# Top-k attention and a GELU MLP in one kernel: q and k turned in 32x32 squares by the vector engine, and top-k over lists of the larger and smaller of key pairs

## The chip, the cores and the metric

The kernel runs on one core of a Trainium2 chip. The core has five engines that run their own instruction queues in order and meet only at semaphores: TensorE (PE; its weight loads are listed as PEld), VectorE (DVE), ScalarE (ACT), GpSimd (POOL) and SyncE (SP, which here only issues DMAs). The metric is the device time of one execution in microseconds, the median over several runs. Lower is better.

## What is computed

Attention over 8 batches, 8 heads, 576 tokens and 64 features, in which every query keeps the 32 largest of its 576 scores; its output, 4608 tokens by 512 features, goes through an MLP with an exact GELU. All data are float32.

```python
scores = scale * np.matmul(q, k.transpose(0, 1, 3, 2))      # (8, 8, 576, 576)
kth = np.partition(scores, -top_k, axis=-1)[..., -top_k:-top_k + 1]   # top_k = 32
mask = scores >= kth
scores = np.where(mask, scores, -1000000000.0)
scores = scores - np.max(scores, axis=-1, keepdims=True)
attn = np.exp(scores)
attn = attn / (np.sum(attn, axis=-1, keepdims=True) + 1e-09)
out = np.matmul(attn, v)
...
x = out.transpose(0, 2, 1, 3).reshape(4608, 512)
h = x @ w_in                                                # (4608, 2048)
g = 0.5 * h * (1.0 + erf(h * inv_sqrt2))
return g @ w_out                                            # (4608, 512)
```

## The kernel before

**Pairs and items.** Two heads of one batch make a pair: 32 pairs, 4 to a batch, so that two heads of 64 features fill 128 partitions. The 576 tokens of a head are four blocks of 128 and a tail of 64 (`NM` = 4, `SM` = 512, `TL` = 64). An item is one block of queries of one pair, both heads side by side (scores of 128 x 1152); the tails of two pairs together make one item more. That gives 18 items a batch, 144 in all. Batches with an even number have their tail items last, the others first.

**Slots.** The main loop (L940 on) runs over slots n. The order of each engine's queue is the order in which the program text issues, written out by hand. In slot n the kernel issues, in this order: the scores of item n+2 (PE, copied to SBUF by ACT), the product of attention and v for item n-3 (PE), the softmax of item n-1 (ACT), the transposes of item n-2's weights (PE, copied by ACT), between them pieces of the MLP (PE), and "prep" pieces that transpose q and k of a later pair; then, at the end of the slot, `top_k(n)` (DVE), `threshold(n)` (POOL), `normalise(n-1)` (POOL) and small additions of the MLP (POOL). From slot 13 on (`few`) the order within a slot is: the tail transposes of item n-2 with the last keys of item n+2, one MLP piece, the other transposes, the first prep piece, the second half of the softmax of item n-1, `add_small(n-1)`, the remaining prep pieces, the rest of the MLP pieces.

**The lines that matter.**

- `load` (L87 to L98) brings q, k or v of one pair to SBUF through SP's queue: four DMAs, two per head, with tokens on the partitions and runs of 64 features. q and k have two buffers each, v five.
- `transpose_qk` (L246 to L273) turns one pair's q and k, features to the partitions, in three pieces: k's four blocks; the two tails; q's four blocks. Each piece is 2 to 4 transposes on PE into a PSUM bank (L263), and a copy by ACT to `kt` or `qm` (L268; the first pair's by DVE). The third piece then issues the loads of the pair two further on. `kt` (tails first, then 512 columns of k) has six buffers, `qm` four. `slots_of` (L928) says in which slot, counted from the batch's first, each piece goes.
- `scores` and `last_keys` (L298 to L362) multiply them; `last_keys` of a tail item is L317.
- `top_k` (L364 to L386) takes the 32 largest of each row: four rounds of MAX8 (L378), which gives the eight largest of 576, and between them three of MATCH_REPLACE8 (L381), which writes a very low number over those eight, each for both heads. After the last MAX8 it issues `inverse(n-1)`, the reciprocal of item n-1's sums (L404).
- `threshold` (L393, L396) makes the two biases of the softmax from the first and the 32nd value; `softmax` (L417, L418) applies them, and its second instruction also sums a row up into `den`; `add_small` (L410) adds 1e-9 to `den`; `normalise` (L431) multiplies with the reciprocals, on POOL in one instruction of 128 x 1152.

So there is a loop from slot to slot: softmax of item n-1, `den`, reciprocal on DVE, `normalise` on POOL, transposes on PE in slot n+1, their copy on ACT, the next softmax behind it on ACT.

- The MLP's first layer is L594, its second L676, L694, L730 and L732, its GELU L610; POOL's part in it is L625 to L628 and L753 to L797. How many of its pieces a slot takes is fixed by `room_in`; it begins at slot 11, as `START` is 10. What is left when the last item is through runs at the end.

Of the kernel before, what the change touches and what calls it, by code (L numbers as in the profile page):

```python
# [8 lines left out]
TOPK = 32  # L9
# [5 lines left out]
def kernel(  # L15
# [55 lines left out]
    xT = const.tile([P, KO, COLS], f32, name="xT")  # L71


    raws = {n: [const.tile([P, NJ, 2, D], f32, name=f"raw_{n}{i}") for i in range(m)]
            for n, m in (("k", 2), ("q", 2), ("v", NP + 1))}
# [11 lines left out]
    def load(n, pair, queue=None, queue2=None):  # L87
        if pair >= n_pairs:
            return
        queue = queue or nc.sync  # L90
        queue2 = queue2 or queue
        b, h0 = pair // NP, 2 * (pair % NP)
        t, src = raw_of(n, pair), sources[n]
# [151 lines left out]

    def transpose_qk(pair, first=False):  # L246

        rq, rk = raw_of("q", pair), raw_of("k", pair)
        groups = {
            0: [(rk, j) for j in range(NM)],  # L250
            1: [(rq, NM), (rk, NM)],
            2: [(rq, j) for j in range(NM)],
        }

        def piece(c):
            if c == 0:
                kt_of[pair] = work.tile([P, 2 * P + SM], f32, tag="kt", bufs=NP + 2, name="kt")
            if c == 2:
                q_of[pair] = work.tile([P, SM], f32, tag="qm", bufs=NP, name="qm")
            tp = bank("tp_qk")  # L260
            n = len(groups[c]) * P
            for x, (r, j) in enumerate(groups[c]):
                nc.tensor.transpose(  # L263
                    tp[:, x * P : (x + 1) * P], r[:, j].rearrange("p e d -> p (e d)"), ident
                )
            dst = q_of[pair] if c == 2 else kt_of[pair][:, 2 * P :] if c == 0 else kt_of[pair][:, 0 : 2 * P]
            copy = nc.vector.tensor_copy if first and c < 2 else nc.scalar.copy
            copy(out=dst, in_=tp[:, 0:n])  # L268
# [29 lines left out]
    def last_keys(i, t_ps):  # L298

        pair, t = items[i]  # L300
        s = S_of[i]
        if t < NM:
            nc.tensor.matmul(  # L303
                t_ps[:, 0:P], lhsT=q_of[pair][:, t * P : (t + 1) * P],
                rhs=kt_of[pair][:, P : 2 * P], start=True, stop=True,
            )
            if i == 0:
                return lambda: nc.vector.tensor_scalar(
                    s[:, SM : S + TL], t_ps[:, 0:P], scale, None, op0=ALU.mult
                )  # L310
            return lambda: nc.scalar.activation(
                s[:, SM : S + TL], t_ps[:, 0:P], func=AF.Copy, scale=scale
            )
        for r in range(2):
            kt = kt_of[pair + r]
            for e in range(2):
                nc.tensor.matmul(  # L317
                    t_ps[half(r, e), r * TL : (r + 1) * TL],
                    lhsT=kt[:, e * TL : (e + 1) * TL],
                    rhs=kt[:, P + e * TL : P + (e + 1) * TL],  # L320
                    start=True, stop=True,
                )
        return lambda: nc.scalar.activation(
            s.rearrange("p (r n) -> p r n", r=2)[:, :, SM:S],
            t_ps[:, 0:P].rearrange("p (r n) -> p r n", r=2), func=AF.Copy, scale=scale,
        )

    def scores(i):
        if i >= N:
            return  # L330
        pair, t = items[i]
        S_of[i] = s = work.tile([P, 2 * S], f32, tag="s", bufs=5, name="s")
        s_ps = pair_tile("s_ps")
        if not few[0]:
            last_keys(i, bank("t_ps"))()
        if t < NM:
            q_t, kt = q_of[pair][:, t * P : (t + 1) * P], kt_of[pair]
            for c in range(2):
                for e in range(2):
                    rows = slice(e * D, (e + 1) * D)  # L340
                    nc.tensor.matmul(  # L341
                        s_ps[:, e, c * 256 : (c + 1) * 256], lhsT=q_t[rows, :],
                        rhs=kt[rows, 2 * P + c * 256 : 2 * P + (c + 1) * 256], start=True, stop=True,
                    )
            if i == 0:

                nc.scalar.activation(s[:, 0:SM], s_ps[:, 0], func=AF.Copy, scale=scale)  # L347
                nc.scalar.activation(s[:, S + TL :], s_ps[:, 1], func=AF.Copy, scale=scale)  # L348
                return
            nc.scalar.activation(spread(s, S + TL, SM), s_ps, func=AF.Copy, scale=scale)  # L350
        else:

            for r in range(2):
                kt = kt_of[pair + r]
                for e in range(2):
                    rows = slice(e * D, (e + 1) * D)
                    nc.tensor.matmul(  # L357
                        s_ps[half(r, e), r, :], lhsT=kt[rows, e * TL : (e + 1) * TL],
                        rhs=kt[rows, 2 * P :], start=True, stop=True,
                    )  # L360
# [3 lines left out]
    def top_k(i, hooks):  # L364


        stat_of[i] = st = {
            "top": work.tile([P, 2, TOPK], f32, tag="top", name="top"),
            "neg": work.tile([P, 2, 2], f32, tag="neg", name="neg"),
            "bias": work.tile([P, 2], f32, tag="bias", name="bias"),  # L370
            "den": work.tile([P, 2], f32, tag="den", name="den"),
            "rden": work.tile([P, 2], f32, tag="rden", name="rden"),
        }
        cur = [row(i, e) for e in range(2)]
        rest = work.tile([P, 2, S], f32, tag="rest", bufs=1, name="rest")
        for r in range(TOPK // 8):
            for e in range(2):
                nc.vector.max(st["top"][:, e, 8 * r : 8 * r + 8], cur[e])  # L378
            if r < TOPK // 8 - 1:
                for e in range(2):  # L380
                    nc.vector.match_replace(  # L381
                        rest[:, e], st["top"][:, e, 8 * r : 8 * r + 8], cur[e], LOWEST
                    )
                cur = [rest[:, e] for e in range(2)]
            if r in hooks:
                hooks.pop(r)()  # L386

    def threshold(i):

        if i < 0 or i >= N:  # L390
            return
        st = stat_of[i]
        nc.gpsimd.tensor_scalar(  # L393
            st["neg"], st["top"][:, :, 0 :: TOPK - 1], -1.0, None, op0=ALU.mult
        )
        nc.gpsimd.tensor_tensor(  # L396
            st["bias"], st["neg"][:, :, 0], st["neg"][:, :, 1], op=ALU.subtract
        )

    def inverse(i):  # L400
        if i < 0 or i >= N:
# [10 lines left out]
    def softmax(i, e):  # L412

        if i < 0 or i >= N:
            return
        st, s = stat_of[i], row(i, e)
        nc.scalar.activation(s, s, func=AF.Prelu, bias=st["neg"][:, e, 1:2], scale=1.0, alpha=STEEP)  # L417
# [101 lines left out]
    def attend(i):  # L519
# [420 lines left out]
    for n in range(ahead):  # L940
# [78 lines left out]
        run_small(6)  # L1019
# [7 lines left out]
        if n <= NP:  # L1027
            load("v", n)

    ready[0], left[0] = NT, len(pieces)  # L1030
# [36 lines left out]
```

## Time and profile before

| what | before |
|---|---|
| median of 3 runs | 1609.99 us (1609.68 to 1610.74) |
| the profiled execution | 1609.49 us |
| its span in the profile | 1607.7 us |
| PE clock granted, mean | 0.996 |
| L594 PE, first layer | 560.7 us, x2560 |
| L378 DVE MAX8, 128x576 | 811.5 us, x1152, 743 and 748 ns each |
| L381 DVE MATCH_REPLACE8, 128x576 | 635.4 us, x864, 743 and 744 ns each |
| L263 PE transposes of q and k | 56.8 us, x320 |
| L268 ACT copies of them | 18.7, 18.1 and 11.5 us |
| L431 POOL `normalise` | 293.0 us, x139, 2108 ns each |
| L404 DVE reciprocal | 22.8 us, x144, and 112.4 us idle before it, for POOL's `den` L410 |
| q and k loads on SP's queue | x64 and x62 of 128 KB, as many of 16 KB, landing after 2.1 to 2.5 us |

"Busy" of a group is the time in which at least one of its instructions runs; as neighbours overlap on DVE and PE, it is less than their number times the mean. Idle time before a group is put down to what ended it. A float32 matmul has two records in the trace, so the numbers of PE's groups for the products are twice those in the program.

### The profile page before, as it was taken

How to read it: one execution, taken by the hardware profiler on the slowest of the kernel's cores; microseconds unless marked ns; L12 is line 12 of the kernel's file. 1: busy time of each engine (PE TensorE's matmuls, PEld its weight loads, DVE VectorE, ACT ScalarE, POOL GpSimd, SP SyncE). 2: the span in 40 equal slices, each digit the busy share in tenths (PEclk: the TensorE clock that was granted, in tenths of full speed). 3: DMA queues.
4: the chain of work that ended last, by engine and by line, in shares of the span. 5: the costliest groups of instructions: out<-in, count | busy, mean ns of one | idle time of the engine just before them, and what ended most of it. 6: DMA issues, size and time to landing. Idle time of an engine off the chain costs nothing.

```text
span 1607.7 us, 27629 instructions
## 1 busy us (share of the span) xinstructions
PE 1568.1 (98%) x10032; PEld 1262.7 (79%) x10032; DVE 1415.5 (88%) x3052; ACT 1205.0 (75%) x2122; POOL 774.1 (48%) x1044
## 2 busy tenths in 40 slices
PE   7899999999999999999999999999999999999998
PEld 6776678888787778888787778888878777888787
DVE  8999989989999889998999888998999988999800
ACT  6989877777778777777777877777777877777730
POOL 4775766534544445433454535443454444543442
PEclk9999999999999999999999999999999999999999
DMA  6523210011100110011110111001110011000000
GB/s 167 150 92 115 83 43 1 14 37 38 23 14 16 43 41 19 1 29 37 31 29 16 29 30 44 1 14 37 38 23 14 16 29 23 14 1 14 8 14 13
DMA packets 126920, 56.31 MB, mean 35 GB/s; under 512 B 117792, under 2 KB 118336, under 8 KB 126784
## 3 DMA queue, kind: packets, MB, share of 16 engines
q1 hardware_dynamic: 125520, 54.12, 12.5%
q8 instruction: 79, 1.29, 0.3%
q10 hardware_dynamic: 1200, 0.39, 0.1%
q14 instruction: 57, 0.47, 0.1%
q0 software_dynamic: 64, 0.03, 0.0%
HBM read 45.08 MB, written 9.44 MB: 34 GB/s over the span
## 4 chain that ended last, share of the span: by engine, by line
PE 89%; DVE 9%; ACT 2%; POOL 1%; issue 0%; DVEq 0%; POOLq 0%
PE h_ps L594 31%; PE y_ps L732 19%; PE o L538 8%; PE s_ps L341 7%; PE tp L481 7%; DVE top L378 5%; DVE rest L381 4%; PE seven L730 3%; PE tp_qk L263 2%; PE tp_t L303 2%; PE y_ps L694 2%; PE y_ps L697 2%; PE y_ps L676 2%; PE s_ps L357 1%; PE o L549 1%; PE tp_t L455 1%
## 5 line engine op out<-in xcount | busy, mean ns | idle before, releaser
L378 DVE MAX8 top<-rest 128x8 f32<-128x576 f32 x864 | 609.7, 748 | 0.0
L594 PE MATMUL h_ps<-xT,w_in_sb 128*128 128x256 f32 (+1 forms) x2560 | 560.7, 363 | 1.0 <-ACT g L610 1.0
L594 PEld LDWEIGHTS h_ps<-xT,w_in_sb 128*128 128x128 f32 x2560 | 428.8, 190 | 82.6 <-issue 32.3
L381 DVE MATCH_REPLACE8 rest<-top,rest 128x576 f32<-128x576 f32 x576 | 423.6, 743 | 0.0
L410 POOL TENSOR_SCALAR den<-den 128x2 f32<-128x2 f32 x144 | 32.0, 222 | 656.3 <-ACT s L418 656.2
L431 POOL TENSOR_TENSOR s<-s,rden 128x1152 f32<-128x1152 f32 x139 | 293.0, 2108 | 0.3 <-DVE rden L404 0.3
L418 ACT ACTIVATE s<-s,bias 128x576 f32<-128x576 f32 x288 | 223.4, 776 | 12.6
L417 ACT ACTIVATE s<-s,neg 128x576 f32<-128x576 f32 x288 | 224.4, 779 | 0.1
L381 DVE MATCH_REPLACE8 rest<-top,s 128x576 f32<-128x576 f32 x288 | 211.8, 744 | 0.0
L497 ACT COPY pt<-tp 128x1024 f32<-128x1024 f32 x133 | 134.5, 1011 | 97.2 <-PE tp L481 96.9
L378 DVE MAX8 top<-s 128x8 f32<-128x576 f32 x288 | 201.8, 743 | 1.4 <-ACT s L347 1.4
L350 ACT ACTIVATE s<-s_ps 128x1024 f32<-128x1024 f32 x127 | 130.4, 1027 | 73.9 <-PE s_ps L341 62.0
L538 PE MATMUL o<-pt,raw_v 128*64 128x256 f32 x1280 | 154.3, 386 | 0.4 <-ACT pt L488 0.4
L481 PE MATMUL tp<-ident,s 128*128 128x128 f32 x1152 | 149.6, 273 | 0.0
L341 PE MATMUL s_ps<-kt,qm 64*128 64x256 f32 x1024 | 147.1, 406 | 0.8 <-ACT s L348 0.8
L481 PEld LDWEIGHTS tp<-ident,s 128*128 128x128 f32 x1152 | 134.6, 141 | 14.8 <-issue 2.1
L732 PE MATMUL y_ps<-w_out_sb,sum 128*128 128x256 f32 x480 | 142.8, 379 | 0.0
L538 PEld LDWEIGHTS o<-pt,raw_v 128*64 128x64 f32 x1280 | 87.1, 137 | 63.9 <-issue 19.9
L341 PEld LDWEIGHTS s_ps<-kt,qm 64*128 64x128 f32 x1024 | 89.1, 188 | 45.4 <-issue 27.1
L732 PE MATMUL y_ps<-w_out_sb,g 128*128 128x256 f32 x480 | 122.5, 379 | 0.0
L404 DVE RECIPROCAL rden<-den 128x2 f32<-128x2 f32 x144 | 22.8, 159 | 112.4 <-POOL den L410 111.9
L732 PEld LDWEIGHTS y_ps<-w_out_sb,sum 128*128 128x128 f32 x480 | 91.2, 190 | 12.4
(132 smaller groups left out, 2176.2 us busy)
## 6 DMA issues: line engine op xcount, KB each, us to landing
raw_q<-in_q_dram SPq DMA_DIRECT2D x64, 128.0 KB, 2.4
raw_v<-in_v_dram SPq DMA_DIRECT2D x64, 128.0 KB, 2.4
raw_k<-in_k_dram SPq DMA_DIRECT2D x62, 128.0 KB, 2.5
out_dram<-y SPq DMA_DIRECT2D x30, 256.0 KB, 2.1
w_out_sb<-in_moe_w_in_dram SPq DMA_DIRECT2D x14, 511.8 KB, 4.9
w_out_sb<-in_moe_w_out_dram SPq DMA_DIRECT2D x10, 511.8 KB, 4.3
w_sum<-in_moe_w_out_dram SPq DMA_DIRECT2D x6, 511.8 KB, 4.3
out_dram<-y SPq DMA_DIRECT2D x11, 128.0 KB, 2.3
```

The source lines that it names most:

```text
L341: nc.tensor.matmul(s_ps[:, e, c * 256 : (c + 1) * 256], lhsT=q_t[rows, :], rhs=kt[rows, 2 * P + c * 256 : 2 * P + (c + 1) * 256], start=Tr ...
L350: nc.scalar.activation(spread(s, S + TL, SM), s_ps, func=AF.Copy, scale=scale)
L378: nc.vector.max(st["top"][:, e, 8 * r : 8 * r + 8], cur[e])
L381: nc.vector.match_replace(rest[:, e], st["top"][:, e, 8 * r : 8 * r + 8], cur[e], LOWEST)
L417: nc.scalar.activation(s, s, func=AF.Prelu, bias=st["neg"][:, e, 1:2], scale=1.0, alpha=STEEP)
L418: nc.scalar.activation(s, s, func=AF.Exp, bias=st["bias"][:, e : e + 1], scale=1.0, accum_out=st["den"][:, e : e + 1],)
L431: nc.gpsimd.tensor_tensor(s, s, wide, op=ALU.mult)
L481: nc.tensor.transpose(tp[:, j * P : (j + 1) * P], s[:, first + j * P : first + (j + 1) * P], ident)
L497: nc.scalar.copy(out=pt_now[0][:, 0 : 2 * NM, x : x + P], in_=tp.rearrange("p e (j n) -> p (e j) n", j=NM),)
L538: nc.tensor.matmul(o[e * D : (e + 1) * D, 0:n], lhsT=vt[:, j, e, :], rhs=pt[:, e * NM + j if j < NM else 2 * NM, :], start=(j == 0), stop= ...
L594: nc.tensor.matmul(h_tile(u)[:, i, :], lhsT=w_in_sb[:, ko, f * P : (f + 1) * P], rhs=xT[:, ko, c0 : c0 + n], start=(ko == 0), stop=(ko == ...
L732: nc.tensor.matmul(acc[names][:, k], lhsT=lhsT, rhs=rhs, start=(j == 0 and k == 0), stop=(j == FT // 2 - 1 and k == 1),)
```

## The change

It has two parts, and some that follow from them.

**Squares.** From pair 8 on (`SQUARES`, batch 2) `load` brings q and k in runs of 32 features, so that square (c, d) of a head, 32 tokens by 32 features, lies in the 32 partitions that its features will have, with the token inside the square on the partition and the feature on the column: 8 DMAs for each of q and k instead of 4. DVE's `transpose`, which exchanges rows and columns within each 32x32 square, then gives `kt` and `qm` directly, in three instructions of 640 columns (k with its tail), 128 (q's tail) and 512 (q), in the same slots as the pieces of before. PE's transposes and ACT's copies of these pairs are gone. In `kt` the 512 columns of k now come first, then k's tail, then q's; pairs 0 to 7 are still turned by PE.

**Lists of pairs.** From item 28 on (`PAIRED`) a row's 576 scores are taken as 288 pairs, key j with key j+288. POOL adds the bit patterns of the two halves as int32 (`sum_up(n+2)`, at the end of slot n behind `normalise`); DVE takes the larger of each pair (`larger(n+1)`, before the last prep pieces and `top_k(n)` of slot n); POOL takes the larger's bit pattern from the sum, which leaves the smaller's (`smaller(n+1)`, before `add_small(n-1)`). `top_k` then runs four rounds over the 288 larger and two over the 288 smaller ones, replacing between the rounds of a list: 12 MAX8 and 8 MATCH_REPLACE8 of 288 instead of 8 and 6 of 576. The 32nd of all comes from the two sorted lists: the maximum of places 17 to 32 of the larger with the 16 of the smaller read backwards, and the least of those 16. These two instructions stand behind the reciprocal of item n-1.

**What follows.** The list tiles take two buffers of 128 x 1152, so v has four buffers instead of five, and each v load is for the pair four further on. `threshold` reads the first and the 32nd value from two tiles; each of its two instructions reads DVE's results directly.

```diff
-            for n, m in (("k", 2), ("q", 2), ("v", NP + 1))}
+            for n, m in (("k", 2), ("q", 2), ("v", NP))}
+    flat = {n: [t.rearrange("p j e d -> p (j e d)") for t in raws[n]] for n in "kq"}
...
+    SQUARES = 2 * NP
...
+        if n != "v" and pair >= SQUARES:
+            t = flat[n][pair % 2]
+            for e in range(2):
+                for d in range(2):
+                    rows, cols = slice((2 * e + d) * SQ, (2 * e + d + 1) * SQ), slice(d * SQ, (d + 1) * SQ)
+                    for at, lo, hi, by in ((0, 0, SM, queue), (SM + e * TL, SM, S, queue2)):
+                        by.dma_start(
+                            out=t[rows, at : at + hi - lo].rearrange("i (c j) -> i c j", j=SQ),
+                            in_=src[b, h0 + e, lo:hi, cols].rearrange("(c i) j -> i c j", i=SQ),
+                        )
+            return
...
+    PAIRED = START + 18
...
+        def squares(c):
+            rq, rk, kt = flat["q"][pair % 2], flat["k"][pair % 2], kt_of[pair]
+            if c == 0:
+                nc.vector.transpose(kt[:, 0:q_tail], rk)
+            elif c == 1:
+                nc.vector.transpose(kt[:, q_tail:], rq[:, SM:])
+            else:
+                nc.vector.transpose(q_of[pair], rq[:, 0:SM])
...
+            (squares if pair >= SQUARES else by_pe)(c)
...
+    def larger(i):
+
+        if paired(i):
+            nc.vector.tensor_tensor(lists_of[i][:, 0], *halves_of(i), op=ALU.max)
+
+    def sum_up(i):
+
+        if paired(i):
+            lists_of[i] = t = work.tile([P, 2, 2, HS], f32, tag="lists", name="lists")
+            a, b = halves_of(i)
+            nc.gpsimd.tensor_tensor(
+                t[:, 1].bitcast(i32), a.bitcast(i32), b.bitcast(i32), op=ALU.add
+            )
+
+    def smaller(i):
+
+        if paired(i):
+            both, top = lists_of[i][:, 1].bitcast(i32), lists_of[i][:, 0].bitcast(i32)
+            nc.gpsimd.tensor_tensor(both, both, top, op=ALU.subtract)
...
+        if paired(i):
+            t = lists_of.pop(i)
+            rounds = [(t[:, 0], t[:, 0], x) for x in into]
+            rounds += [(t[:, 1], t[:, 1], low[:, :, 8 * r : 8 * r + 8]) for r in range(half_k // 8)]
+            ends = (len(into) - 1, len(rounds) - 1)
...
+        for r, (src, dst, x) in enumerate(rounds):
             for e in range(2):
-                nc.vector.max(st["top"][:, e, 8 * r : 8 * r + 8], cur[e])
...
+                nc.vector.max(x[:, e], src[:, e])
+            if r not in ends:
                 for e in range(2):
...
+                    nc.vector.match_replace(dst[:, e], x[:, e], src[:, e], LOWEST)
+            if r == len(rounds) - 1:
+                last()
...
+        nc.vector.tensor_tensor(upper, upper, backwards, op=ALU.max)
+        nc.vector.tensor_reduce(
+            st["kth"].rearrange("p (e x) -> p e x", x=1), upper, mybir.AxisListType.X, ALU.min
+        )
...
+        nc.gpsimd.tensor_scalar(st["neg"], st["kth"], -1.0, None, op0=ALU.mult)
+        nc.gpsimd.tensor_tensor(st["bias"], st["kth"], st["first"][:, :, 0], op=ALU.subtract)
...
-                load("v", pair + r + NP + 1)
+                load("v", pair + r + NP)
...
             softmax(n - 1, 1)
+        larger(n + 1)
+        smaller(n + 1)
         add_small(n - 1)
...
-            top_k(n, {3: lambda: inverse(n - 1)})
+            top_k(n, lambda: inverse(n - 1))
...
         normalise(n - 1, 2 if on_pool(u) else 0)
+        sum_up(n + 2)
```

More of the change, by code (lines that the diff above doesn't have):

```diff
@@ L71 @@
     xT = const.tile([P, KO, COLS], f32, name="xT")
+    SQ = 32
     raws = {n: [const.tile([P, NJ, 2, D], f32, name=f"raw_{n}{i}") for i in range(m)]
-            for n, m in (("k", 2), ("q", 2), ("v", NP + 1))}
+            for n, m in (("k", 2), ("q", 2), ("v", NP))}
+    flat = {n: [t.rearrange("p j e d -> p (j e d)") for t in raws[n]] for n in "kq"}
     nc.gpsimd.memset(raws["k"][0][:, NM], 0.0)
@@ L92, in load @@
         b, h0 = pair // NP, 2 * (pair % NP)
-        t, src = raw_of(n, pair), sources[n]
+        src = sources[n]
+        if n != "v" and pair >= SQUARES:
[9 more added lines that the diff above has]
+            return
+        t = raw_of(n, pair)
         for e in range(2):
@@ L246, in transpose_qk, with by_pe @@
     def transpose_qk(pair, first=False):
[L248 to L253, printed above, removed]
+        q_tail, k_tail = SM + P, SM
+        def squares(c):
[6 more added lines that the diff above has]
+                nc.vector.transpose(q_of[pair], rq[:, 0:SM])
+        def by_pe(c):
+            rq, rk = raw_of("q", pair), raw_of("k", pair)
+            group = (
+                [(rk, j) for j in range(NM)], [(rk, NM), (rq, NM)], [(rq, j) for j in range(NM)]
+            )[c]
+            tp = bank("tp_qk")
+            for x, (r, j) in enumerate(group):
+                nc.tensor.transpose(
+                    tp[:, x * P : (x + 1) * P], r[:, j].rearrange("p e d -> p (e d)"), ident
+                )
+            dst = (kt_of[pair][:, 0:SM], kt_of[pair][:, SM:], q_of.get(pair))[c]
+            copy = nc.vector.tensor_copy if first and c < 2 else nc.scalar.copy
+            copy(out=dst, in_=tp[:, 0 : len(group) * P])
         def piece(c):
@@ L259, in piece @@
                 q_of[pair] = work.tile([P, SM], f32, tag="qm", bufs=NP, name="qm")
[L260 to L268, printed above, removed]
+            (squares if pair >= SQUARES else by_pe)(c)
             if c == 2:
@@ L304, in last_keys @@
                 t_ps[:, 0:P], lhsT=q_of[pair][:, t * P : (t + 1) * P],
-                rhs=kt_of[pair][:, P : 2 * P], start=True, stop=True,
+                rhs=kt_of[pair][:, SM : SM + P], start=True, stop=True,
             )
@@ L318, in last_keys @@
                     t_ps[half(r, e), r * TL : (r + 1) * TL],
-                    lhsT=kt[:, e * TL : (e + 1) * TL],
-                    rhs=kt[:, P + e * TL : P + (e + 1) * TL],
+                    lhsT=kt[:, SM + P + e * TL : SM + P + (e + 1) * TL],
+                    rhs=kt[:, SM + e * TL : SM + (e + 1) * TL],
                     start=True, stop=True,
@@ L342, in scores @@
                         s_ps[:, e, c * 256 : (c + 1) * 256], lhsT=q_t[rows, :],
-                        rhs=kt[rows, 2 * P + c * 256 : 2 * P + (c + 1) * 256], start=True, stop=True,
+                        rhs=kt[rows, c * 256 : (c + 1) * 256], start=True, stop=True,
                     )
@@ L357, in scores @@
                     nc.tensor.matmul(
-                        s_ps[half(r, e), r, :], lhsT=kt[rows, e * TL : (e + 1) * TL],
-                        rhs=kt[rows, 2 * P :], start=True, stop=True,
+                        s_ps[half(r, e), r, :], lhsT=kt[rows, SM + P + e * TL : SM + P + (e + 1) * TL],
+                        rhs=kt[rows, 0:SM], start=True, stop=True,
                     )
@@ L362, in scores, with paired, halves_of, top_k @@
             nc.scalar.activation(s2[:, :, 0:SM], s_ps, func=AF.Copy, scale=scale)
-    def top_k(i, hooks):
+    lists_of = {}
+    HS = S // 2
+    def paired(i):
+        return PAIRED <= i < N
+    def halves_of(i):
+        s = S_of[i].rearrange("p (e h n) -> p e h n", e=2, h=2)
+        return s[:, :, 0], s[:, :, 1]
+    def larger(i):
[12 more added lines that the diff above has]
+            nc.gpsimd.tensor_tensor(both, both, top, op=ALU.subtract)
+    def top_k(i, last):
         stat_of[i] = st = {
-            "top": work.tile([P, 2, TOPK], f32, tag="top", name="top"),
-            "neg": work.tile([P, 2, 2], f32, tag="neg", name="neg"),
+            "first": work.tile([P, 2, 8], f32, tag="first", name="first"),
+            "kth": work.tile([P, 2], f32, tag="kth", name="kth"),
+            "neg": work.tile([P, 2], f32, tag="neg", name="neg"),
             "bias": work.tile([P, 2], f32, tag="bias", name="bias"),
@@ L373, in top_k @@
         }
-        cur = [row(i, e) for e in range(2)]
-        rest = work.tile([P, 2, S], f32, tag="rest", bufs=1, name="rest")
-        for r in range(TOPK // 8):
+        half_k = TOPK // 2
+        top = work.tile([P, 2, TOPK - 8], f32, tag="top", bufs=1, name="top")
+        low = work.tile([P, 2, half_k], f32, tag="low", bufs=1, name="low")
+        into = [st["first"]] + [top[:, :, 8 * r : 8 * r + 8] for r in range(TOPK // 8 - 1)]
+        if paired(i):
[3 more added lines that the diff above has]
+            ends = (len(into) - 1, len(rounds) - 1)
+        else:
+            s = S_of[i].rearrange("p (e n) -> p e n", e=2)
+            t = work.tile([P, 2, S], f32, tag="lists", name="rest")
+            rounds = [(s if r == 0 else t, t, x) for r, x in enumerate(into)]
+            ends = (len(rounds) - 1,)
+        for r, (src, dst, x) in enumerate(rounds):
             for e in range(2):
-                nc.vector.max(st["top"][:, e, 8 * r : 8 * r + 8], cur[e])
-            if r < TOPK // 8 - 1:
+                nc.vector.max(x[:, e], src[:, e])
+            if r not in ends:
                 for e in range(2):
[L381 to L386, printed above, removed]
+                    nc.vector.match_replace(dst[:, e], x[:, e], src[:, e], LOWEST)
+            if r == len(rounds) - 1:
+                last()
+        if not paired(i):
+            st["kth"] = top[:, :, TOPK - 9]
+            return
+        upper = top[:, :, half_k - 8 :]
+        backwards = bass.AP(
+            tensor=low.tensor, offset=low.offset + half_k - 1,
+            ap=[list(low.ap[0]), [half_k, 2], [-1, half_k]],
+        )
+        nc.vector.tensor_tensor(upper, upper, backwards, op=ALU.max)
+        nc.vector.tensor_reduce(
+            st["kth"].rearrange("p (e x) -> p e x", x=1), upper, mybir.AxisListType.X, ALU.min
+        )
     def threshold(i):
@@ L392, in threshold @@
         st = stat_of[i]
[L393 to L398, printed above, removed]
+        nc.gpsimd.tensor_scalar(st["neg"], st["kth"], -1.0, None, op0=ALU.mult)
+        nc.gpsimd.tensor_tensor(st["bias"], st["kth"], st["first"][:, :, 0], op=ALU.subtract)
     def inverse(i):
@@ L416, in softmax @@
         st, s = stat_of[i], row(i, e)
-        nc.scalar.activation(s, s, func=AF.Prelu, bias=st["neg"][:, e, 1:2], scale=1.0, alpha=STEEP)
+        nc.scalar.activation(s, s, func=AF.Prelu, bias=st["neg"][:, e : e + 1], scale=1.0, alpha=STEEP)
         nc.scalar.activation(
@@ L1026 @@
                 load_weights(m)
-        if n <= NP:
+        if n < NP:
             load("v", n)
```

## The prediction

> **What bounds it now.** First the shares of the page and its chain of waits.
>
> ```profile
> PE 1568.1 (98%) x10032; PEld 1262.7 (79%) x10032; DVE 1415.5 (88%) x3052; ACT 1205.0 (75%) x2122; POOL 774.1 (48%) x1044
> PE 89%; DVE 9%; ACT 2%; POOL 1%; issue 0%; DVEq 0%; POOLq 0%
> ```
>
> PE is nearly never idle and carries the chain; DVE comes second. Shares are averages, so I next cut the span at the reciprocals (L404), of which each slot has one. Slots 0 to 12 last 9.70 us each and are DVE's own. Slot 28, the first that the change reaches in earnest, begins at 296.45. The table by stretch of that part: PE, PEld, DVE, ACT, POOL busy; then L263 (the q/k transposes) alone, PE and PEld.
>
> ```profile
> 296.45:1532.68 1236.23, 1222.72 (x7822) 989.87 (x7819) 1133.15 (x2438) 946.83 (x1684) 554.45 (x809) 1.00 0.09 23
> ...
> 296.45:1532.68 1236.23, 38.47 (x240) 29.93 (x240) 1.00 0.09 23
> ```
>
> In these 117 slots PE idles 13.5 us in all, so PE bounds them. But 42 of the slots last 9.7 us with no wait in DVE's queue, the others 10.2 to 13.3 with DVE waiting for `den`: DVE has only some 0.85 us to spare per slot. After 1532.68 only the MLP is left (75 us, PE). The timeline around one reciprocal shows the loop that ties the engines:
>
> ```profile
> 817.40 0.17 DVE L404 RECIPROCAL rden<-den 128x2 f32<-128x2 f32 x1 [1.44 <-POOL den L410]
> 817.45 0.23 POOL L393 TENSOR_SCALAR neg<-top 128x4 f32<-128x4 f32 x1
> 817.48 1.40 DVE L378 MAX8 top<-s 128x8 f32<-128x576 f32 x2
> 817.76 0.20 POOL L396 TENSOR_TENSOR bias<-neg 128x2 f32<-128x2 f32 x1
> 817.90 2.11 POOL L431 TENSOR_TENSOR s<-s,rden 128x1152 f32<-128x1152 f32 x1
> ...
> 818.80 0.07 DVE L381 MATCH_VALUE_LOAD rest<-top,s 128x8 f32 x1
> 818.86 0.74 DVE L381 MATCH_REPLACE8 rest<-top,s 128x576 f32<-128x576 f32 x1
> ...
> 819.52 0.08 DVE L381 MATCH_VALUE_LOAD rest<-top,s 128x8 f32 x1
> ...
> 820.94 0.27 PE L455 MATMUL tp_t<-ident,s 128*128 128x128 f32 x1
> ```
>
> Reciprocal to end of `normalise` is 2.62 us, and PE needs its result 0.92 us after that. Over the 117 slots this slack is 0.48 to 5.2 us.
>
> **What leaves PE and ACT.** 24 pairs' transposes: 38.5 us of PE (row above), and before them PE waits 5.4 us for the copies of the group in front, by the waits of that stretch (the one bank "z"). With them go 72 ACT copies, 36.9 us, which ACT (946.8 of 1236) didn't lack. PE's own sum falls by 43.9 us in 63 slots, 0.7 each.
>
> **DVE per slot.** From the starts above: a MAX8 every 0.66 us, a load with replace every 0.72. Now 8 x 0.66 + 6 x 0.725 + 0.08 = 9.71, which is the short slot. The reciprocal's step is 0.08 for two elements, so 0.06 is fixed and 1.04 ns is one element. At 288: MAX8 0.36, replace with its load 0.43. After: 12 x 0.36 + 8 x 0.425 = 7.72; the maximum (576 elements, two inputs) 0.66; reciprocal, the 2x16 maximum and the reduction some 0.45 with their dependence: 8.85 us. Bounds: 7.7 (fixed part hidden) to 9.5 (0.1 more on each of the small ones). Transposes of 640, 128 and 512 columns: no row shows one. Nearest below is L435's stream, 576 in 0.45 us (1.0 us a pair), above two passes at MAX8's rate (2.8); I take one pass: 0.73 + 0.19 + 0.59 = 1.5, as a 32x32 exchange has one input like MAX8. So DVE has 8.85 in plain slots and 9.0 to 9.6 with a transpose, under PE's 10.0 there (those slots last 10.7 now, less 0.7): the saving of DVE pays for the transposes and buys nothing itself, save in the last two slots (9.70, DVE's own): -1 us.
>
> **The loop's length.** `kth` now comes after the reciprocal, through two small instructions: +0.4 us before `neg`. Then `larger` of the next item goes first on DVE and reads two SBUF inputs while POOL wants to read. What the trace has of that is DVE's two-port scaling beside POOL in slot 14:
>
> ```profile
> 146.46 0.23 POOL L393 TENSOR_SCALAR neg<-top 128x4 f32<-128x4 f32 x1 [1.58 <-DVE rden L404]
> 146.54 0.95 DVE L435 TENSOR_SCALAR s<-s,rden 128x576 f32<-128x576 f32 x2
> 146.77 0.35 POOL L396 TENSOR_TENSOR bias<-neg 128x2 f32<-128x2 f32 x1
> ```
>
> `bias` takes 0.35 for 0.20: held, but done before the second scaling. I take +0.3, 0.7 in all. Summing what exceeds each slot's slack gives 3.6 us for +0.7, 0.35 for +0.4, 16.3 for +1.1 (a whole `larger` in front).
>
> The Trainium skill, "SBUF — State Buffer", section "Who interferes with whom", is harsher: a two-input DVE instruction and a POOL instruction that reads SBUF exclude each other, and the first holds the read port to its end. The row agrees that POOL is held, though not for DVE's whole pair; by the rule the loop costs 16 us in place of 3.6 and the first rival below holds.
>
> **POOL.** Two int32 additions of 576 per item. L202, 1024 elements, takes 2.41, L625, 256 elements, 0.73: by the line between, 1.44 each, 2.9 per slot; bounds 2.1 (half of L431's 1152 elements in 2.11 us, twice) and 3.3 (L625's rate, twice 1.64). They go into POOL's wait for `den`, 1.5 to 8.2 us per slot. Where it is under 4.4 (2.9, the loop's 0.7, shorter slots) `den` comes late: 12 us in a period of 36 slots, 39 in all, if nothing else had slack. The slots after the tight ones have mostly 2 to 3 us, so I take 4 (0 to 39).
>
> **Waits moved to DVE.** A `kt` buffer serves again six pairs later. Three times (pairs 14, 22, 30) the new piece stands in the very slot in which PE last reads the old tile; in slot 50:
>
> ```profile
> 534.29 0.45 PE L317 MATMUL tp_t<-kt 128*64 128x64 f32 x8
> ```
>
> DVE is there at 528.9, so its queue stands 5.8 us, with the whole top-k behind it, where formerly only PE and ACT, which come later, met this. DVE would end at 534.8 + 0.73 + 0.66 + 0.19 + 7.72 = 544.1, against the 540.6 of before less 1.6 for the removed transposes: 5.1 late, less 1.8 slack: 3.3 us, 10 for three (0 if DVE's lag is made up, 17 at most). The other pieces' buffers were read last at least one slot before.
>
> **DMA, at nothing.** 16 loads a pair in place of 8, each about 0.55 us on SP's queue: 9 us, landing 2.4 later, against two slots (20 us) at the closest from issue to use. Packets of q and k double, 55,000 more on engines 9% busy. If the cover went, DVE would stand for the load at the head of a slot. The v load goes into the buffer just freed as before; it is needed one pair sooner, at the closest 1.5 slots (15 us) after issue for 7 us of loads.
>
> **Sum.** 1607.7 - 43.9 - 1 + 3.6 + 4 + 10 = 1580.4 of span. The profiled run was 1609.49, 1.8 over its span, the median 0.5 over that: 1583.
>
> **Rivals.**
> *POOL shuts `larger` out (slower).* In 42 of the 63 slots with transposes a 640 or 512 wide one stands before `larger` in DVE's queue. By then (0.5 us after `kth`) POOL has `neg` and `bias` behind it and starts `normalise`, 2.11 us. If DVE can't read beside it, `larger` waits 1.9, and that slot of DVE is 8.85, 0.66 for the transpose and 1.9, 11.4 together, against PE's 10.0: 59 us over 42 slots, some 44 if a quarter falls into slack: 1627. For: `bias` stretched to 0.35. Against: it was let in before DVE was done. It decides from 0.64 us per wide slot, where the 27 us are gone.
> *Everything is hidden.* Long slots absorb the late `kth`, `den` and `kt`: 1607.7 - 44.9 + 2.3 = 1565. For: mean slack over 2 us. Against: 0.48 in the short ones.
> *POOL's queue sets `den`.* The 39 us fall due: 1618. For: 1.5 us idle in the tightest slots. Against: it idles over 4 us in most.
> *The lists bring a wait by tile.* If `larger` had to await `sum_up` in the same tile, DVE would lose some 3.5 us per slot, near 1900. Against: ACT writes columns of `xT` (L543 at 810.07) while PE reads others.
>
> **Chances.** Forecast 0.52 (1570 to 1600), all hidden 0.15, POOL shuts out 0.21, POOL's queue 0.09, tile 0.03. Range 1558 to 1622: below, PE's remaining idle also goes; above, half the first rival. 0.2% (3.2 us) is what a measurement can tell: faster 0.70, same 0.05 (the edge of the first and third rival), slower 0.25.
>
> **What would show it.** L263 at 80 matmuls; MAX8 of 288 near 0.45 us long; the transposes near 0.75, 0.2, 0.65; DVE's slots without a wait near 8.9, 9.6 with a wide piece, not 11.4; `larger` starting at once behind a transpose; a DVE wait of some 6 us for PE at L317 in slots 50, 86, 122; `den` still put down to ACT. A `larger` that starts when `normalise` ends, or PE idle far over 13.5 us, makes the forecast wrong.

## The result and the profile after

| kernel | median | runs | ratio to before, 95% interval |
|---|---|---|---|
| before | 1609.84 us | 4 (1609.52 to 1610.74) | |
| after | 1621.11 us | 4 (1619.66 to 1622.80) | 1.0069 [1.0052, 1.0087] |

The change makes the kernel 0.7% slower. The profiled execution took 1622.80 us, its span is 1621.0, and its mean granted clock is 0.986 where the kernel before had 0.996.

The first line of the page lists the engines' busy time. PE has lost 10.0 us, ACT 32, POOL has gained 368; DVE's sum hasn't moved, although its shortest slots went from 9.70 to 8.80 us.

```profile
PE 1558.1 (96%) x9792; PEld 1251.9 (77%) x9792; DVE 1414.5 (87%) x4399; ACT 1172.7 (72%) x2050; POOL 1141.6 (70%) x1276
```

The groups of instructions say why DVE's sum stands still. The columns are busy time, mean ns of one, and idle time of the engine before them.

```profile
L404 DVE TENSOR_TENSOR lists<-s 128x576 f32<-128x576 f32 x116 | 152.5, 1315 | 0.0
L473 POOL TENSOR_SCALAR neg<-kth 128x2 f32<-128x2 f32 x116 | 48.6, 419 | 139.8 <-DVE kth L464 137.1
```

`larger` takes 1315 ns in the mean, and a second view gives the median as 749 ns and the largest as 2602. It has no idle time in front of it: a held instruction counts as busy. The same work takes one of several times, depending on what stands beside it. Of the 116, 42 take 1.2 us or more, 37 of them 2.2 or 2.6. `neg`, two numbers per partition, takes 419 in the mean.

The timeline of a slot with a 512 wide transpose ahead of `larger` (start, duration, engine, line):

```profile
802.02 0.17 DVE L480 RECIPROCAL rden<-den 128x2 f32<-128x2 f32 x1 [1.02 <-POOL den L486]
...
802.30 0.19 DVE L464 TENSOR_REDUCE kth<-top 128x2 f32<-128x32 f32 x1
802.41 0.70 DVE L273 STREAM_TRANSPOSE qm<-raw_q 128x512 f32<-128x512 f32 x1
802.57 0.22 POOL L473 TENSOR_SCALAR neg<-kth 128x2 f32<-128x2 f32 x1 [0.59 <-DVE kth L464]
802.76 0.20 POOL L474 TENSOR_TENSOR bias<-kth,first 128x2 f32<-128x2 f32 x1
802.91 2.11 POOL L507 TENSOR_TENSOR s<-s,rden 128x1152 f32<-128x1152 f32 x1
803.03 2.60 DVE L404 TENSOR_TENSOR lists<-s 128x576 f32<-128x576 f32 x1
804.98 1.93 POOL L411 TENSOR_TENSOR lists<-s 128x576 int32<-128x576 int32 x1
```

While DVE transposes, POOL runs through `neg` and `bias` and starts `normalise` at 802.91, 0.12 before `larger`. `normalise` keeps its 2.11 us; `larger` needs until 805.63, that is 0.61 after `normalise` has ended. Then the roles change: `sum_up` (L411), 1.41 when alone, comes in while `larger` reads, and takes 1.93. Where no wide transpose stands ahead, `larger` is first:

```profile
813.30 0.15 DVE L480 RECIPROCAL rden<-den 128x2 f32<-128x2 f32 x1
...
813.64 0.19 DVE L464 TENSOR_REDUCE kth<-top 128x2 f32<-128x32 f32 x1
813.75 0.75 DVE L404 TENSOR_TENSOR lists<-s 128x576 f32<-128x576 f32 x1
813.91 0.66 POOL L473 TENSOR_SCALAR neg<-kth 128x2 f32<-128x2 f32 x1 [2.39 <-DVE kth L464]
814.54 0.19 POOL L474 TENSOR_TENSOR bias<-kth,first 128x2 f32<-128x2 f32 x1
814.69 2.10 POOL L507 TENSOR_TENSOR s<-s,rden 128x1152 f32<-128x1152 f32 x1
```

Now `larger` keeps its 0.75 and `neg` is held for it, 0.66 in place of 0.22.

**Where the time went.** Cut at the reciprocals as in the prediction, slots 28 to 144 take 1247.08 us, against 1236.23 before. By kind of slot (42 with a wide transpose ahead of `larger`, 21 others with a transpose, 54 without):

| slots | before | after |
|---|---|---|
| 42 wide | 449.0 us, 10.69 each | 488.6 us, 11.63 each |
| 21 other | 230.8, 10.99 | 210.7, 10.03 |
| 54 plain | 556.4, 10.30 | 547.8, 10.14 |

The loss lies in the wide slots alone; the others gained. Of the 42, 24 last 11.28 to 11.35 us, and DVE stands 0.2 us at most in each of them: this is its own length with a held `larger`.

The same stretch by engine (length, then busy time of PE, PEld, DVE, ACT, POOL, clock, DMA share, GB/s):

```profile
297.25:1544.33 1247.08, 1210.29 (x7576) 977.63 (x7573) 1130.71 (x3785) 913.70 (x1611) 919.68 (x1039) 0.99 0.11 24
```

PE idles 36.8 us here, where it was 13.5. Its busy time fell by only 12.4, though 240 matmuls are gone. The clock shows the reason. Slot 50 as it is in the timeline, and the table of 5 us stretches behind it:

```profile
536.61 0.45 PE L343 MATMUL tp_t<-kt 128*64 128x64 f32 x8
...
536.99 0.84 DVE L269 STREAM_TRANSPOSE kt<-raw_k 128x640 f32<-128x640 f32 x1 [3.20 <-PE tp_t L343]
...
549.95 0.48 PE L531 MATMUL tp_t<-ident,s 128*128 128x128 f32 x1 [4.11 <-POOL s L507]
```

```profile
540.00:545.00 5.00, 5.00 (x27) 3.47 (x26) 5.00 (x19) 3.04 (x6) 2.55 (x4) 1.00 0.11 18
545.00:550.00 5.00, 0.89 (x12) 0.42 (x11) 4.97 (x12) 1.64 (x3) 2.55 (x4) 0.82 0.09 15
550.00:555.00 5.00, 5.00 (x17) 4.26 (x18) 5.00 (x16) 1.56 (x4) 3.19 (x2) 0.50 0.46 74
555.00:560.00 5.00, 5.00 (x32) 3.23 (x32) 4.96 (x20) 4.72 (x7) 0.71 (x3) 1.00 0.19 31
```

DVE stands 3.20 us for PE's last reading of the old `kt` tile, its queue behind it is late, the next `larger` is held, and in the next slot PE waits 4.11 us for `s`. For the 5 us after that PE has half its clock. Six such waits occur, three of 4.11 and three of 2.29; the kernel before has none over 1.5 us between 200 us and the MLP's last pieces.

### The profile page after: what moved, and what is told of

Same layout as the page of the kernel before. It is cut to its first block, busy times and chain, and to the rows that moved or that the text cites. A ratio compares the mean times of both kernels' runs of the same rounds, so it can differ in the third digit from the quotient of the medians.

```text
span 1621.0 us, 28936 instructions
## 1 busy us (share of the span) xinstructions
PE 1558.1 (96%) x9792; PEld 1251.9 (77%) x9792; DVE 1414.5 (87%) x4399; ACT 1172.7 (72%) x2050; POOL 1141.6 (70%) x1276
## 5 line engine op out<-in xcount | busy, mean ns | idle before, releaser
L448 DVE MAX8 top<-lists 128x8 f32<-128x288 f32 x696 | 280.8, 443 | 0.0
L451 DVE MATCH_REPLACE8 lists<-top,lists 128x288 f32<-128x288 f32 x464 | 201.0, 439 | 0.0
L448 DVE MAX8 low<-lists 128x8 f32<-128x288 f32 x464 | 186.3, 441 | 0.0
L411 POOL TENSOR_TENSOR lists<-s 128x576 int32<-128x576 int32 x116 | 183.7, 1584 | 0.0
L419 POOL TENSOR_TENSOR lists<-lists 128x576 int32<-128x576 int32 x116 | 163.7, 1411 | 3.8
L557 PE MATMUL tp<-ident,s 128*128 128x128 f32 x1152 | 154.5, 278 | 0.0
L404 DVE TENSOR_TENSOR lists<-s 128x576 f32<-128x576 f32 x116 | 152.5, 1315 | 0.0
L473 POOL TENSOR_SCALAR neg<-kth 128x2 f32<-128x2 f32 x116 | 48.6, 419 | 139.8 <-DVE kth L464 137.1
L808 PE MATMUL y_ps<-w_out_sb,g 128*128 128x256 f32 x480 | 127.3, 391 | 0.0
```

What stands on the lines that cost most here:

```text
L411: nc.gpsimd.tensor_tensor(t[:, 1].bitcast(i32), a.bitcast(i32), b.bitcast(i32), op=ALU.add)
L419: nc.gpsimd.tensor_tensor(both, both, top, op=ALU.subtract)
L448: nc.vector.max(x[:, e], src[:, e])
L451: nc.vector.match_replace(dst[:, e], x[:, e], src[:, e], LOWEST)
L557: nc.tensor.transpose(tp[:, j * P : (j + 1) * P], s[:, first + j * P : first + (j + 1) * P], ident)
L808: nc.tensor.matmul(acc[names][:, k], lhsT=lhsT, rhs=rhs, start=(j == 0 and k == 0), stop=(j == FT // 2 - 1 and k == 1),)
```

## The experiments

Line numbers in the fences are those of each kernel, some lines off the change's. Ratios are to the kernel before, which was measured again beside each group (medians 1609.78 us for the first four, 1609.87 for the next four, 1610.69 for the three after, 1611.12 for the last).

| kernel | median us | ratio, 95% interval | clock |
|---|---|---|---|
| `larger` ahead of the prep pieces | 1592.21 | 0.9888 [0.9873, 0.9902] | 0.992 |
| `larger` with one input | 1597.97 | 0.9920 [0.9904, 0.9937] | 0.987 |
| lists alone | 1616.27 | 1.0040 [1.0025, 1.0055] | 0.997 |
| squares alone | 1597.72 | 0.9922 [0.9908, 0.9937] | 0.993 |
| `larger` early, three pairs a slot later | 1577.71 | 0.9801 [0.9786, 0.9815] | 0.996 |
| `larger` ahead of the reciprocal | 1592.46 | 0.9893 [0.9878, 0.9908] | 0.992 |
| the same, three pairs a slot later | 1577.08 | 0.9795 [0.9781, 0.9810] | 0.996 |
| lists alone, `larger` ahead of the reciprocal | 1611.35 | 1.0003 [0.9994, 1.0013] | 0.995 |
| the change, three pairs a slot later | 1620.61 | 1.0049 [1.0031, 1.0068] | 0.987 |
| squares alone, three pairs a slot later | 1582.05 | 0.9815 [0.9799, 0.9832] | 0.995 |
| before, three pairs a slot later | 1614.77 | 1.0019 [1.0010, 1.0028] | 0.996 |
| before, no q/k transposes from pair 8 on | 1577.31 | 0.9793 [0.9777, 0.9809] | 0.995 |

The theory after the result: DVE's two-input `larger` and POOL's readings of SBUF exclude each other for whole instructions, and the wide transposes decide who is first. The rivals: the longer loop, POOL's additions, the wait for `kt`.

**1. `larger` first, the transposes behind it.** No instruction is added or taken away.

```diff
+        larger(n + 1)
         for x, piece in enumerate(now):
...
-        larger(n + 1)
         smaller(n + 1)
```

> larger(n+1) is issued ahead of the first transpose of the slot instead of behind it; nothing else moves. Theory A (DVE's two-input maximum and POOL's normalise exclude each other, and behind a 640 or 512 wide transpose POOL is first): larger takes 0.75 us everywhere instead of 2.2 to 2.6 behind a transpose, the slots with a wide transpose fall from 11.3 to 9.4 to 9.8 where PE lets them, the time to 1575 to 1590, and the granted clock rises again from 0.986 to 0.99 or more, as PE waits less for normalise. Theory B (DVE has simply too much work in these slots: transposes of 0.85, 0.30 and 0.70 us where 0.73, 0.19 and 0.59 were reckoned): the work is the same, 1615 to 1621. Theory C (POOL's three microseconds more per slot make den late): the same, 1615 to 1621.

1592.21 us, 29 less than the change, a little more than the upper end expected; the wide slots last 10.65 us. Its groups:

```profile
L404 DVE TENSOR_TENSOR lists<-s 128x576 f32<-128x576 f32 x116 | 86.9, 749 | 0.0
L473 POOL TENSOR_SCALAR neg<-kth 128x2 f32<-128x2 f32 x116 | 75.8, 654 | 95.4 <-DVE kth L464 84.4 <-PE y_ps L808 6.1 <-PE s_ps L367 5.0
```

`larger` now takes 0.75 everywhere and `neg` 0.65 in the mean. The loss has gone to the other side: there `neg` is held for `larger` by 0.44, where `larger` was held for `normalise` by 1.85. The order costs 29 us.

**2. `larger` as an instruction with one input**, a reduction over the pairs, in the change's place behind the transposes.

```diff
-            nc.vector.tensor_tensor(lists_of[i][:, 0], *halves_of(i), op=ALU.max)
+            pairs = S_of[i].rearrange("p e (h n) -> p e n h", e=2, h=2)
+            nc.vector.tensor_reduce(
+                lists_of[i][:, 0].rearrange("p e (n x) -> p e n x", x=1), pairs, mybir.AxisListType.X, ALU.max
+            )
```

> larger stays where it is, behind the first transpose, but is one reduction over pairs (1152 elements read as one input) instead of a maximum of two inputs; the same values. Theory A: it takes some 1.2 to 1.3 us everywhere and does not wait for normalise; POOL's neg is 0.22 us again instead of 0.66; slots with a wide transpose 10.0 to 10.2 instead of 11.3; the time 1585 to 1600 although DVE has 0.5 us more work in each of 116 slots. Theory B: DVE gets fuller by 58 us in all, so slower than the changed kernel: 1630 to 1670. If the wait belonged to the queue or a semaphore and not to the read port, the reduction would still end with normalise and the time would be 1620 or more.

```profile
L405 DVE TENSOR_REDUCE lists<-s 128x576 f32<-128x1152 f32 x116 | 157.1, 1354 | 0.0
L476 POOL TENSOR_SCALAR neg<-kth 128x2 f32<-128x2 f32 x116 | 25.6, 220 | 132.4 <-DVE kth L467 128.1 <-PE y_ps L776 4.4
```

1597.97 us: 23 us faster than the change, although this `larger` takes 1354 ns, as long as the held one in the mean, and does so in all slots (1329 to 1382). `neg` is back at 220. So it is neither the place nor DVE's sum but two inputs at once beside a reading POOL. The Trainium skill, "SBUF — State Buffer", section "Who interferes with whom", says that a DVE instruction with at most one SBUF input doesn't contend with GpSimd, outside the two-port modes; these two rows agree.

**3 and 4. One part alone.** Lists without squares, and squares without lists.

```diff
-    SQUARES = 2 * NP
+    SQUARES = n_pairs
```

> All pairs turned by PE and ACT as before; the lists stay. No transpose stands before larger any more. Theory A: larger 0.75 us in all 116 slots; PE has its 44 us back and bounds again, POOL's neg held by larger lengthens the loop a little: 1607 to 1614. Theory B: DVE falls to 8.8 us per slot, PE bounds: 1605 to 1610. Theory C: POOL has the same extra work as in the changed kernel, den is late as there: 1616 to 1622.

```diff
-        return PAIRED <= i < N
+        return False
```

> The squares stay, the lists are left out for all items (top-k over 576 as before). DVE has 9.72 us per slot and 10.0 to 10.6 with a transpose. Theory A: no two-input instruction on DVE, no exclusion; wide slots at 10.5 against 11.3 with the lists: 1590 to 1605. Theory B: transposes are what is too dear; 1605 to 1615. Theory C: POOL is relieved, so well below the changed kernel, like A.

The lists alone cost 6.5 us (1616.27). That is more than the range of theory A, the lock, allowed, and at the lower end of theory C, POOL's additions; experiment 8 decides between them. The top-k's saving on DVE buys nothing there, as foretold. The squares alone bring 12.1 us (1597.72). The two alone would add up to 5.6 us faster, together they are 11 slower: the loss sits in their meeting, in `larger` behind a transpose.

**5. `larger` early, and three pairs' pieces one slot later** (pairs 14, 22, 30), so that DVE writes no `kt` buffer in the slot of its last reading.

```diff
     first = {2: (0, 1, 1), 3: (2, 2, 3)}
+    first.update({b * NP + 2: (-3, -3, -2) for b in range(3, B, 2)})
```

> `larger` early as in the first experiment, and besides it the pieces of the third pair of batches 3, 5 and 7 one slot later, so that DVE no longer writes a `kt` buffer in the slot in which PE last reads it (slots 50, 86, 122). If the remaining loss is this wait with what follows from it (DVE stands 3.7 us, PE then idles up to 3.4 us and some of the MLP's matmuls run at a lower granted clock), three times some 4 us goes: 1578 to 1586 us, no wait of DVE over 1 us for a transpose in these slots, PE's longest wait for `s` under 2 us there, mean clock at 0.994 or over. If long slots absorb the wait anyway (rival), the time stays at 1590 to 1594. If the later piece collides with the reading of the next scores, a new wait of PE for `kt` or `qm` appears and it is over 1595.

1577.71 us, 14.5 below experiment 1 and 0.3 under the range expected. The stretch of slots 28 to 144, first in experiment 1, then here:

```profile
298.52:1516.23 1217.71, 1199.57 (x7576) 970.85 (x7573) 1061.81 (x3785) 911.65 (x1611) 915.99 (x1039) 1.00 0.12 24
```

```profile
297.56:1499.95 1202.39, 1194.35 (x7576) 967.70 (x7573) 1061.48 (x3785) 910.85 (x1611) 915.87 (x1039) 1.00 0.12 24
```

15.3 us less: 10.1 of them are PE's idle time (18.1 to 8.0), 5.2 its busy time, for the same 7576 records. No wait of PE over 1.5 us is left in this stretch, and the granted clock is 0.996 again over the span. The clock is 0.50 for 3.4 us after each of the three waits of experiment 1, and never below 1.00 in these slots here. So one third of what this wait costs is the lower clock after it.

**6 to 8. `larger` in DVE's wait for `den`.** The combination of the two lists and `larger` of item n+2 go ahead of the reciprocal, when POOL is idle; experiment 7 adds the shift, 8 leaves the squares out.

```diff
...
-            if r == len(rounds) - 1:
-                last()
...
+        larger(i + 2)
+        last()
...
-        larger(n + 1)
         smaller(n + 1)
```

> The combination of the two sorted lists (`kth`) and `larger` of item n+2 stand ahead of the reciprocal on DVE, where DVE waits for `den` anyway, and POOL is idle then. So the loop from `den` to `normalise` is as short as in the kernel before (`neg` comes right behind the reciprocal, 0.22 us and not 0.65), and nothing shares the read port. Lock theory: `larger` at 0.75 us in all slots, `neg` at 0.22, some 1 us per slot less in the loop, of which only the tight slots show something: 1582 to 1590 us. If PE bounds nearly all slots already (rival), it is the first experiment's 1590 to 1594. If the reciprocal comes later because DVE has no spare time there (rival), the slots of the transposes grow and it is over 1597.

> Both of these: `kth` and `larger` ahead of the reciprocal, and the three pairs' pieces one slot later. If the gains add up: 1572 to 1582 us, the lowest of all, PE idle under 25 us from slot 28 on. If both touch the same waits: that of the better of the two.

> The lists alone (all q and k turned by PE as before), with `kth` and `larger` ahead of the reciprocal. The lists alone in the change's order measured 1616.3 us against 1609.8. If that loss was the longer loop (0.4 us of `kth` and `neg` held to 0.65 us by `larger`), it goes: 1607 to 1611 us. If it was POOL's two additions (rival), it stays at 1614 to 1618. DVE's saving is worth nothing in either case, as PE bounds these slots.

`normalise` starts 0.38 us after the reciprocal in place of 1.34 (before the change 0.51; all three are medians). With the squares this buys nothing: 1592.46 and 1577.08, where experiments 1 and 5 have 1592.21 and 1577.71. The rival of experiment 6 held, and in 7 the gains did not add up. Without them it matters: 1611.35 in place of 1616.27. So 4.9 of the 6.5 us of experiment 3 were the longer loop. The 1.5 that remain (1611.35 against 1609.87) aren't told apart from nothing: the interval ends at 1.0013, so POOL's two additions cost some 2 us at most here, provided that DVE's saving hides none of it.

**9. The change itself with the shift of experiment 5.**

> The change as it is, with `larger` behind the prep pieces, and only the pieces of the third pair of batches 3, 5 and 7 one slot later. With `larger` early the same shift was worth 14.5 us (1592.2 to 1577.7). If the wait for `kt` and the lock are separate losses that add up: 1604 to 1609 us against the change's 1621. If the lock's own lateness already covers the wait (rival): 1614 to 1621.

1620.61 us: the two losses do not add up, the rival is right. The timeline shows where the wait went. The shifted pieces now stand in slots 51 and 52, ahead of `larger`. The lines are of slot 52, the last one of slot 53:

```profile
555.58 0.70 DVE L273 STREAM_TRANSPOSE qm<-raw_q 128x512 f32<-128x512 f32 x1
...
556.08 2.11 POOL L507 TENSOR_TENSOR s<-s,rden 128x1152 f32<-128x1152 f32 x1
556.20 2.60 DVE L404 TENSOR_TENSOR lists<-s 128x576 f32<-128x576 f32 x1
...
558.72 0.30 DVE L271 STREAM_TRANSPOSE kt<-raw_q 128x128 f32<-128x128 f32 x1
558.95 0.66 DVE L273 STREAM_TRANSPOSE qm<-raw_q 128x512 f32<-128x512 f32 x1
...
570.80 0.48 PE L531 MATMUL tp_t<-ident,s 128*128 128x128 f32 x1 [3.71 <-POOL s L507]
```

Slot 50 shrinks from 13.59 to 9.43 us, but 51, 52 and 53 grow to 12.20, 12.13 and 10.39 (from 12.05, 10.50, 8.80), and PE waits 3.71 us in place of 4.11, two slots later, again with a clock of 0.50 in the 5 us after it. Slots 50 to 54 last 56.5 us in both.

**10 and 11. The shift without the lists, and in the kernel before.**

> The squares alone (top-k over all 576 as before), with the shift of those pieces. The squares alone without the shift measured 1597.7 us. If PE bounds and the lists buy nothing besides DVE's room for the transposes: the shift brings 12 to 15 us here too, 1582 to 1586 us, a little over the 1577.7 with lists, since DVE's slot is then 9.7 and 0.85 or 0.7 of a transpose in it against PE's 10.0. If the lists are needed to make the transposes fit (rival): 1590 us or more.

> A control: the kernel before with the same shift of those pieces, still turned by PE. Here DVE doesn't meet the wait for the `kt` buffer, only PE and ACT do. If the shift's gain is the wait on DVE's queue: no change, 1608 to 1612 us. If the shift is worth something by itself, as a better order of the work (rival): under 1605 us.

Squares alone with the shift: 1582.05, as expected, 4.3 us over experiment 5 (3.5 if each is taken against the kernel before measured beside it). That is all that the lists are worth beside the squares. The kernel before with the shift is 0.19% slower, 3 us outside the range expected: the shift isn't a better order by itself, and its gain belongs to the wait on DVE's queue.

**12. The PE term by itself.** The kernel before, in which q and k of the pairs from 8 on aren't transposed at all (those of batch 1 are used again); nothing takes their place.

```diff
         def piece(c):
+            if pair >= 2 * NP:
+                if c == 2:
+                    load("q", pair + 2)
+                    load("k", pair + 2)
+                (q_of if c == 2 else kt_of)[pair] = (q_of if c == 2 else kt_of)[pair - NP]
+                return
```

> The prediction's PE term by itself: the kernel before, in which the pairs from 8 on use the transposed q and k of batch 1 again, so PE's 240 transposes and ACT's 72 copies of them are left out and nothing is put in their place (the loads stay; the output of batches 2 to 7 isn't the reference's). The prediction's size (38.5 us busy and 5.4 us of waits): 1565 to 1568 us. The size by PE's pitch (240 at 0.109 us, 26.2, and 5.4 of waits: 31.6): 1577 to 1580 us. If DVE's slots of 9.7 us take the lead where PE shrinks (rival): 1583 us or more.

1577.31 us: 33.8 us, and no more, is what all of PE's and ACT's share of the transposes costs. Its page:

```profile
PE 1541.2 (98%) x9792; PEld 1240.7 (79%) x9792; DVE 1414.3 (90%) x3052; ACT 1170.7 (74%) x2050; POOL 774.1 (49%) x1044
```

PE's busy time falls by 26.9 us from 1568.1, not by the 38.5 of L263's row. And the time is that of experiments 5 and 7 within 0.6 us: with the lock and the `kt` wait mended, squares and lists are hidden altogether.

## Why the prediction was wrong

The direction was wrong; the first rival, "POOL shuts `larger` out", is what happens.

**The step that failed** is the reading of slot 14 in the kernel before, "held, but done before the second scaling. I take +0.3", and from it the chance of 0.21 for the first rival. So the sum has no term for `larger` held by `normalise`, where the runs show 28.9 us. The row that was read is of two DVE instructions in 0.95 us, each 0.52 long. The first ends at 147.06 and `bias`, 0.20 long when alone, at 147.12: by these times it was held to the end of one instruction and slipped in before the next. The kernel before has five such slots. In all of them `bias` ends 0.05 or 0.06 us behind the end of the first scaling, and where it starts earliest it takes longest:

```profile
181.18 0.95 DVE L435 TENSOR_SCALAR s<-s,rden 128x576 f32<-128x576 f32 x2
181.27 0.49 POOL L396 TENSOR_TENSOR bias<-neg 128x2 f32<-128x2 f32 x1
```

That is the rule of the Trainium skill quoted there (the holder keeps the read port to its end), not a softer one. And "let in before DVE was done" spoke of a gap between two short instructions; `normalise` is a single one of 2.11 us. The change and experiment 1 show the exclusion from both sides: 2.60 for 0.75 on DVE, 0.66 for 0.22 on POOL; experiment 2, with one input, shows neither.

That 1621.1 lies within the stated range, which ends at 1622 for "half the first rival", doesn't speak for the sum: 28.9 us of the miss are that rival, and 14.6 are two terms with a wrong size. Point by point:

- **The rival's sum** was right in its parts: `larger` held by 1.85 (priced 1.9), 24 of the wide slots at 11.28 to 11.35 (11.4). Its price of 44 us is 42.9 between experiments 9 and 5, but 28.9 between the change and experiment 1, since there the `kt` wait, 14.5 by itself, is covered by the same lateness.
- **PE's term** was mis-sized: -43.9 forecast, -33.8 measured. The 5.4 us of waits are right (in the stretch from slot 28 on PE idles 8.1 us without the transposes, 13.5 with them). The busy time of a group wasn't what leaves: four of these transposes show 0.60 us, with 0.27 for the last one alone, so they start every 0.11 us, which is 26 us for 240; the next matmul can begin inside the rest. From the fall of PE's whole busy time: 26.9.
- **DVE per slot**: plain 8.80 (8.85 forecast); with a wide transpose, `larger` not held, 9.62 (9.6). The transposes take 0.845, 0.30 and 0.70 us, 1.85 a pair (1.5 forecast, one pass for each element; by the three lengths there is a fixed part of some 0.17). That DVE's saving "buys nothing itself" is right. Of the slots read as "10.2 to 13.3", three last 9.94, which changes nothing.
- **The loop**: `normalise` starts 0.83 later after the reciprocal (1.34 to 0.51), 0.7 forecast. In the lists alone it costs 4.9 us (3.6 forecast); beside the squares nothing that experiment 6 against 1 could show.
- **POOL**: 1.41 per addition, 1.44 forecast; 4 us taken, some 2 at most measured (experiment 8).
- **The `kt` wait**: at the three places named, 3.20 us in place of 5.8, as DVE comes later there than before (3.67 in experiment 1); but the loss is 14.5 (10 forecast, 17 at most), since the clock falls after PE's wait, which the sum left out. PE's idle time alone is 10.1.
- **DMA**: waits of DVE for `raw_k` before L269 are 0.6 us in all; forecast nothing.
- **The rival by tile** is refuted: `larger` has no idle time in front of it, so it never waits for `sum_up`. "Everything is hidden" had the right mechanism for the mended kernel, but at 1577, not 1565, because it used the same PE term.

Put together with the measured sizes: the forecast 1583, plus 10.1 for PE, 4.5 for `kt` and 28.9 for the lock, less 7.2 for loop and POOL (the sum had 7.6 for these, and experiment 5 is only 0.4 above 12), is 1619.3; measured 1621.1.

## What to carry to other kernels

Before a two-input DVE instruction is put into a queue, look at what POOL reads at that moment, and from which of the two the next one waits: here `larger` ahead of `neg` costs 0.44 us and `larger` behind the start of `normalise` 1.85. An idle moment of POOL (here DVE's own wait for `den`) mostly costs neither, and a one-input form neither, though it took 1.35 us in place of 0.75 itself. A held instruction shows as a long busy one without idle time, so compare the longest with the median of a group. Price a removed group by what the engine's whole busy time would lose (number times pitch), not by the group's own busy time, and look for waits that a change moves onto an engine in whose queue all the other work stands, as here the wait for `kt`.

## What the runs showed of the hardware

The granted clock falls with the long waits of PE: it is 0.50 in the 5 us stretch behind the wait of 4.11 us, 0.50 in the one that holds the end of that of 3.71 (experiment 9), 0.79 in the one that holds the end of that of 3.38 (experiment 1). The change's six waits, of 4.11 and 2.29, come with 15.9 us of longer busy time over slots 28 to 144 (1210.29 against 1194.35 in experiment 5 for the same 7576 records), besides 28.8 of idle time. In these slots PE is busy for 27.0 us at a clock of 0.50, so some 13.5 of the 15.9 is the clock (an estimate, by halving).

The Trainium skill, "TensorE: Matmul & The Clock Gate", section "What's actually happening", states that the clock is halved after an idle window of about 3.4 us. The traces agree with the length, but PE wasn't idle for all of it. The change's table around a wait of 2.29 us, then around one of 4.11, cut where the clock changes:

```profile
374.09:377.50 3.41, 1.11 (x8) 0.85 (x7) 3.41 (x12) 1.72 (x5) 3.37 (x4) 1.00 0.02 5
377.50:380.91 3.41, 3.41 (x14) 2.95 (x13) 3.41 (x13) 0.64 (x3) 2.31 (x2) 0.50 0.00 0
380.91:384.30 3.39, 3.39 (x18) 2.72 (x16) 2.44 (x11) 3.34 (x5) 0.38 (x2) 1.00 0.00 0
...
544.75:548.17 3.42, 1.08 (x12) 0.59 (x10) 3.39 (x13) 0.71 (x2) 0.72 (x3) 1.00 0.00 0
548.17:551.58 3.41, 1.63 (x5) 1.37 (x6) 3.41 (x4) 1.61 (x5) 3.41 (x2) 0.50 0.40 64
551.58:554.99 3.41, 3.41 (x14) 2.94 (x13) 3.41 (x14) 1.12 (x2) 1.61 (x2) 0.50 0.41 66
554.99:558.40 3.41, 3.41 (x22) 2.46 (x20) 3.41 (x14) 3.35 (x6) 0.22 (x1) 1.00 0.28 46
```

In both, PE was busy 1.1 of the 3.4 us ahead of the fall, and the second wait had lasted 2.3 us when the clock fell. The clock changes in steps of 3.41 us: from 377.50 to 548.17 it is 50 of them. The kernel before has a wait of 2.80 us, ending at 109.20, which takes some of each of two such steps, and there the clock doesn't fall:

```profile
104.20:107.61 3.41, 2.19 (x20) 1.16 (x18) 3.41 (x8) 3.38 (x5) 1.89 (x4) 1.00 0.02 5
107.61:111.02 3.41, 1.82 (x11) 1.65 (x12) 3.41 (x9) 3.29 (x7) 3.41 (x2) 1.00 0.01 2
111.02:114.44 3.42, 3.42 (x22) 2.93 (x20) 3.42 (x9) 2.45 (x6) 3.01 (x3) 1.00 0.00 0
```

So the length of a wait doesn't decide alone: it matters how little PE did in one step. How little is enough wasn't tried.
